# Six places for inputs instead of four in a fused attention, soft-MoE and gate kernel on one core

## The chip, the core and the metric

The kernel runs on one core of one Trainium2 chip. The metric is the device time of one execution in microseconds, as the median of several runs; lower is better. Before the change it is 154.87 us.

## The reference, cut to what matters

Three blocks follow each other: an attention between 512 tokens and 32 states per batch and head (both ways), a soft mixture of experts over all 4352 tokens, and a last block that changes only tokens whose skip score is above zero.

```python
scores = scale * np.matmul(x, state.transpose(0, 1, 3, 2))     # x: 8 batches, 8 heads, 512 x 64
xread = np.matmul(softmax(scores), state)
sread = np.matmul(softmax(scale * np.matmul(state, x.transpose(0, 1, 3, 2))), x)
...
d = softmax over tokens of (x @ phi)                            # phi: 512 x 32
slot_input = d.T @ x
h = np.maximum(slot_input[e] @ w1[e], 0.0)                      # w1: 8 x 512 x 1024
slot_out[e] = h @ w2[e]                                         # w2: 8 x 1024 x 512
out = softmax over slots of (x @ phi) @ slot_out
```

All data is float32. x is 8.4 MB, w1 and w2 are 16.8 MB each, and the output is 8.9 MB; so each byte of the 51.8 MB that cross the DMA queues crosses them once.

## The kernel before, in words

**Three parts.** The attention part handles eight batches, one after the other and interleaved. Then the first layer (`layer1`, line 691) multiplies the gathered slots with the eight `w1` weights, in two groups of four weights (`g` 0: weights 0 to 3, `g` 1: weights 4 to 7) and four quarters `kt` each; the second layer (`layer2`, line 775) does the same with `w2`, in sixteen units of 1 MB; and `combine` (line 805) and `store` (line 830) make and write the output.

**The order is written out by hand.** `ORDER` (line 556) is a list of steps, each a name with a batch or weight and a half, quarter or head; every engine gets its instructions in the order of that list. `A` are the transposes of an input on TensorE and `evA` their eviction, `Sc` the scores, `Tr`, `Er` and `aTr` other transposes, `R` the state's read (the last step of a batch that reads its input), `Lg` and `G` the logits and the gathering, `Bc` and `Dr` small transposes; `evS`, `sp`, `addT`, `mnT`, `sumT`, `evR` run on VectorE, `exS`, `exE`, `exT`, `evA` on ScalarE, `subT`, `nrmT`, `mvR` on GpSimd. `ldx.b.h` loads four heads of input b (0.5 MB), `ldw.n.q` quarter q of first-layer weight n (0.5 MB), `ldv` and `ldv2` units or half units of `w2`.

**All loads stand on one queue.** SyncE issues every load in the list's order. An issue waits until the place that it writes is free, and what stands behind it waits too. Each issue also waits for the completion of the issue eight before it, so that at most eight transfers are under way.

**Places.** An input takes 2048 words per partition. Inputs have four places: `XA` and `XB` in the working memory, and the two halves of the region of weight 7 (`w67[:, 4096:8192]`).

```python
w1s = [at(4096 * n, 4096) for n in range(6)] + [w67[:, 0:4096], w67[:, 4096:8192]]
xslot = [0, 1, 2, 3, 0, 1, 2, 0]
base = [XB, XT0, S0, XA, STT0, A0]        # w2 units 0 to 5
```

So input 4 waits for `R.0`, input 5 for `R.1`, input 6 for `R.2` and input 7 for `R.4`; weight 7 is loaded when inputs 6 and 3 are done. The first six units of `w2` go to the attention's working memory (`base`) as it comes free, the other ten where the first layer has used up quarters of `w1` (`w2u`, line 176).

Of the kernel before, what the change touches and what calls it, by code (L numbers as in the profile page):

```python
# [17 lines left out]
def kernel(  # L18
# [535 lines left out]


    ORDER = """
        ldsb.1.0 ldsb.0.0 warm.7.0 cp.0.0 cp.1.0 ST.1.0 cp.0.1 ldx.0.6 cp.1.1 ldx.0.0 ST.1.1 ldx.0.2 ST.0.0 phi.0.0
        ST.0.1 ldx.1.0 evST.1.0 evST.1.1 A.0.0 evST.0.0 A.0.3 evST.0.1 A.0.1 A.0.2 evA.0.3.dve evA.0.0.act
        evA.0.2.act Q.0.0 evA.0.1.act sh.0.0 ldx.1.4 sh.1.0 evsh.0.0 evQ.0.0 Sc.0.0 A.1.0 A.1.1 evS.0.0 evA.1.0.act
        evS.0.1 sp.0.1 ldx.2.4 A.1.2 sp.0.0 evA.1.1.act ldx.2.0 Bc.0.0 evsh.1.0 ldx.3.4 evB.0.0 Tr.0.1 A.1.3 Tr.0.0  # L560
        evA.1.2.act exE.0.1 evA.1.3.act addT.0.1 exE.0.0 Q.1.0 Sc.1.0 exS.0.1 R.0.0 mnT.0.1 ldx.3.0 evQ.1.0 addT.0.0
        mnT.0.0 ldx.4.0 exS.0.0 evS.1.1 A.2.0 sp.1.1 evS.1.0 subT.0.1 subT.0.0 A.2.1 exT.0.1 A.2.2 exT.0.0
        evA.2.1.act evA.2.0.act Bc.1.0 sp.1.0 evA.2.2.act A.2.3 sumT.0.0 Tr.1.0 evB.1.0 sumT.0.1 evA.2.3.act exS.1.0
        Tr.1.1 eps.0.0 rec.0.0 nrmT.0.0 ldx.4.4 A.3.0 Sc.2.0 A.3.2 exS.1.1 nrmT.0.1 addT.1.1 evR.0.0 evA.3.0.act
        mnT.1.1 evS.2.0 aTr.0.0 ldw.4.0 ldw.5.0 evA.3.2.act A.3.3 aTr.0.1 evaT.0.0 evS.2.1 addT.1.0 sp.2.0
        evA.3.3.act Bc.2.0 evaT.0.1 evB.2.0 A.3.1 mnT.1.0 subT.1.1 subT.1.0 Lg.0.0 ldw.3.0 A.4.0 sp.2.1 evA.3.1.act
        exE.1.0 exT.1.1 exE.1.1 exT.1.0 evL.0.0 Tr.2.0 Sc.3.0 sumT.1.1 R.1.0 exL.0.0 sumT.1.0 eps.1.0 ldw.0.0 Tr.2.1
        ldw.2.0 evA.4.0.act ldw.6.0 Dr.0.0 exS.2.0 rec.1.0 A.4.1 evD.0.0 nrmT.1.0 exS.2.1 ldw.1.0 A.4.2 evR.1.0
        nrmT.1.1 ldx.5.4 ldw.1.1 evA.4.1.act G.0.0 evS.3.0 evA.4.2.act evS.3.1 addT.2.1 mnT.2.1 ldx.5.0 evG.0.0
        addT.2.0 aTr.1.0 subT.2.1 evaT.1.0 aTr.1.1 evaT.1.1 A.4.3 evA.4.3.act RT.0.0 Bc.3.0 evB.3.0 evRT.0.0 mnT.2.0  # L570
        Lg.1.0 ldw.6.1 Sc.4.0 evL.1.0 sp.3.1 ldw.3.1 A.5.2 exT.2.1 sp.3.0 Tr.3.1 exE.2.0 Tr.3.0 subT.2.0 exL.1.0
        Dr.1.0 exT.2.0 exE.2.1 exS.3.1 A.5.0 sumT.2.1 A.5.1 mvR.0.0 sumT.2.0 eps.2.0 rec.2.0 evD.1.0 nrmT.2.1
        ldw.5.1 exS.3.0 ldw.0.1 nrmT.2.0 R.2.0 evA.5.2.act G.1.0 evA.5.0.act ldx.6.0 evA.5.1.act ldw.4.1 A.5.3
        evS.4.1 sp.4.1 evR.2.0 evS.4.0 addT.3.1 evG.1.0 aTr.2.1 evA.5.3.act ldx.6.4 aTr.2.0 evaT.2.1 ldw.2.1
        evaT.2.0 Tr.4.1 Lg.2.0 exS.4.1 mvR.1.0 mnT.3.1 Bc.4.0 addT.3.0 subT.3.1 exT.3.1 A.6.0 mnT.3.0 evL.2.0
        ldw.4.2 sp.4.0 exL.2.0 evB.4.0 Dr.2.0 sumT.3.1 subT.3.0 exT.3.0 sumT.3.0 eps.3.0 evD.2.0 rec.3.0 nrmT.3.0
        exE.3.0 Sc.5.0 exE.3.1 G.2.0 R.3.0 ldw.2.2 RT.1.0 nrmT.3.1 evG.2.0 addT.4.1 evA.6.0.act Tr.4.0 mnT.4.1
        ldw.6.2 ldw.3.2 RT.2.0 evRT.1.0 aTr.3.0 aTr.3.1 evR.3.0 ldw.1.2 A.6.3 addT.4.0 ldw.0.2 evRT.2.0 exS.4.0
        mnT.4.0 evaT.3.0 subT.4.1 evaT.3.1 evS.5.0 exT.4.1 Lg.3.0 sp.5.0 ldw.5.2 subT.4.0 exE.4.0 evL.3.0 exL.3.0
        Tr.5.0 exT.4.0 Dr.3.0 evS.5.1 Bc.5.0 sumT.4.1 evD.3.0 exE.4.1 evB.5.0 sumT.4.0 mvR.2.0 evA.6.3.act A.6.2  # L580
        exS.5.0 eps.4.0 R.4.0 rec.4.0 G.3.0 nrmT.4.0 sp.5.1 addT.5.0 ldx.7.4 evA.6.2.act ldx.7.0 nrmT.4.1 A.6.1
        Tr.5.1 evG.3.0 evA.6.1.act exS.5.1 aTr.4.0 mnT.5.0 addT.5.1 RT.3.0 mnT.5.1 aTr.4.1 evaT.4.0 Sc.6.0 subT.5.0
        evaT.4.1 exT.5.0 evR.4.0 Lg.4.0 evRT.3.0 A.7.3 evS.6.0 evS.6.1 evL.4.0 exE.5.0 subT.5.1 sp.6.1 exT.5.1
        sumT.5.1 A.7.2 A.7.1 exL.4.0 sumT.5.0 Dr.4.0 eps.5.0 Tr.6.1 mvR.4.0 exE.5.1 mvR.3.0 Bc.6.0 rec.5.0 evD.4.0
        nrmT.5.0 evA.7.2.act sp.6.0 A.7.0 R.5.0 evB.6.0 evA.7.1.act G.4.0 ldw.3.3 evR.5.0 ldw.0.3 Tr.6.0 addT.6.1
        ldw.2.3 ldw.5.3 mnT.6.1 ldw.4.3 nrmT.5.1 addT.6.0 evA.7.3.act evA.7.0.act ldw.1.3 mnT.6.0 exS.6.1 RT.5.0
        aTr.5.0 subT.6.1 evRT.5.0 exS.6.0 RT.4.0 ldw.6.3 mvR.5.0 aTr.5.1 Sc.7.0 evaT.5.0 evaT.5.1 Lg.5.0 exT.6.1
        evS.7.0 evL.5.0 Ls.0.0 exE.6.0 evS.7.1 Tr.7.0 evRT.4.0 evLs.0.0 ldv.4.0 exL.5.0 exE.6.1 sumT.6.1 subT.6.0
        Dr.5.0 exT.6.0 ldv.0.0 R.6.0 mnT.7.0 evD.5.0 sumT.6.0 evG.4.0 eps.6.0 ldw.7.0 ldw.7.1 rec.6.0 nrmT.6.0 G.5.0
        subT.7.0 ldw.7.2 ldw.7.3 exS.7.0 exS.7.1 warm.2.0 Tr.7.1 exT.7.0 Er.7.0 evR.6.0 mnT.7.1 RT.6.0 Er.7.1  # L590
        epsR.7.0 evE.7.0 subT.7.1 evE.7.1 evG.5.0 aTr.6.0 exT.7.1 R.7.0 recR.7.0 nrmT.6.1 evRT.6.0.dve sumT.7.0
        evR.7.0 mvR.6.0 sumT.7.1 epsT.7.0 aTr.6.1 epsT.7.1 recT.7.1 warm.4.0 recT.7.0 evaT.6.0 RT.7.0 nrmT.7.0.dve
        evaT.6.1 ldv2.2.0 Lg.6.0 nrmT.7.1 evRT.7.0 Ls.1.0 aTr.7.0 evLs.1.0 evL.6.0 evaT.7.0.dve ldv2.3.0 ldv2.4.1
        exL.6.0 aTr.7.1 mvR.7.0 Dr.6.0 LsT.0.0 evaT.7.1 evD.6.0 Lg.7.0 evL.7.0 exL.7.0 G.6.0 still.0.0 ldv2.5.0
        Dr.7.0 ldv2.2.1 evD.7.0 rowmax.0.0 G.7.0 exLs.0.0 still.0.0 exW.0.0 evG.6.0 esT.0.0 U.0.0 evG.7.0 ldv2.5.1
        evEs.0.0 U.1.0 sip0.0.0 wsg.0.0 ldv2.1.0 evU.0.0 evU.1.0 ldv2.1.1 SI.0.0 evSI.0.0 siT.0.0 evsi.0.0
# [462 lines left out]
```

## Time and profile before

| | |
|---|---|
| three runs | 154.41, 154.87, 155.14 us; median 154.87 us |
| profiled execution, its own time | 155.36 us |
| its span, first to last instruction | 153.5 us |
| PE, DVE, ACT, POOL busy | 130.0, 96.3, 84.8, 50.7 us |
| bytes moved, mean rate over the span | 51.84 MB, 338 GB/s |

The time of a run is that of the whole program; the span leaves out what lies ahead of the first and behind the last instruction, here 1.9 us. Starts in the rows are counted from the span's start. GB/s is what the core's 16 DMA engines moved together, and the DMA share is how busy they were on the mean; a share a little over 1 is a full stretch.

### The profile page before, as it was taken

To read this page: it belongs to the slowest core of one execution; us is meant where nothing else is said; L and a number is where in the kernel's file an instruction comes from. 1 tells how busy PE (TensorE), PEld (TensorE's weight loads), DVE (VectorE), ACT (ScalarE), POOL (GpSimd) and SP (SyncE) were. 2 spreads that over 40 slices of the span, in tenths; PEclk is the share of its full clock that TensorE was granted. 3 is DMA by queue.
4 is the path that set the end of the run, shared out by engine and by line. 5 is a ranking of instruction groups with operands and counts; after the bars stand their busy time and mean duration, and the time that the engine had idled before them with its cause. 6 is when DMAs were issued, how large, how long until landed. Compare 5 with 4: busy or idle time off the path is not lost.

```text
span 153.5 us, 4807 instructions
## 1 busy us (share of the span) xinstructions
PE 130.0 (85%) x1950; PEld 82.3 (54%) x1950; DVE 96.3 (63%) x230; ACT 84.8 (55%) x200; POOL 50.7 (33%) x89
## 2 busy tenths in 40 slices
...
PEclk9999999999999999999999999999999999999755
DMA  3999379999989999999899999999999689999980
GB/s 147 312 322 363 114 249 417 409 337 396 378 290 366 413 410 365 408 406 427 305 342 416 364 348 351 397 408 413 374 348 348 221 274 335 338 344 328 373 337 17
DMA packets 27916, 51.84 MB, mean 338 GB/s; under 512 B 2272, under 2 KB 19696, under 8 KB 27248
## 3 DMA queue, kind: packets, MB, share of 16 engines
...
HBM read 42.55 MB, written 8.91 MB: 335 GB/s over the span
## 4 chain that ended last, share of the span: by engine, by line
PE 51%; DMA 17%; DVE 14%; ACT 4%; issue 3%; POOL 2%; SPq 1%; ACTq 0%; DVEq 0%; POOLq 0%
PE b L243 11%; DMA mem<-in_x_dram 10%; PE b L784 7%; PE b L817 5%; PE pair L696 5%; PE b L696 5%; DMA mem<-in_moe_w_dram 4%; PE b L361 3%; DMA w<-in_x_dram 3%; PE pair L258 3%; DVE mem L266 3%; PE b L519 2%; DVE mem L319 2%; DVE mem L285 1%; PE b L719 1%
## 5 line engine op out<-in xcount | busy, mean ns | idle before, releaser
L239 ACT COPY mem<-b 128x512 f32<-128x512 f32 (+2 forms) x88 | 39.9, 506 | 23.4 <-PE b L797 7.9
L243 PE MATMUL b<-mem 128*128 128x128 f32 x240 | 34.1, 285 | 6.2 <-DMA mem<-in_x_dram 4.8
L243 PEld LDWEIGHTS b<-mem 128*128 128x128 f32 x240 | 27.6, 146 | 12.0 <-DMA mem<-in_x_dram 5.3
L327 POOL TENSOR_TENSOR mem<-mem 128x512 f32<-128x512 f32 x14 | 14.8, 1063 | 20.1 <-DVE mem L319 19.9
L347 POOL TENSOR_TENSOR mem<-mem 128x512 f32<-128x512 f32 x15 | 16.2, 1098 | 15.8 <-DVE mem L343 11.7
L784 PE MATMUL b<-mem 128*32 128x256 f32 (+1 forms) x208 | 16.4, 431 | 0.3
L784 PEld LDWEIGHTS b<-mem 128*32 128x32 f32 x208 | 6.7, 110 | 9.0 <-issue 4.8
L266 DVE TENSOR_SCALAR_CACHE_REDUCE mem<-pair 128x512 f32<-128x512 f32 x16 | 10.7, 680 | 1.4 <-PE pair L258 0.7
L817 PE MATMUL b<-mem 32*128 32x256 f32 (+1 forms) x72 | 11.3, 468 | 0.2
L331 ACT ACTIVATE mem<-mem 128x512 f32<-128x512 f32 x16 | 10.2, 640 | 2.0 <-POOL mem L327 1.2
L337 DVE TENSOR_REDUCE mem<-mem 128x16 f32<-128x512 f32 x16 | 10.4, 676 | 1.0 <-ACT mem L331 1.0
L300 DVE TENSOR_TENSOR mem<-b,mem 128x512 f32<-128x512 f32 x14 | 9.5, 678 | 1.1 <-ACT mem L307 0.6
L381 POOL COPY mem<-mem 32x128 f32<-32x128 f32 x32 | 9.7, 302 | 1.4
L319 DVE TENSOR_REDUCE mem<-mem 128x16 f32<-128x512 f32 x14 | 9.6, 684 | 0.4
L285 DVE TENSOR_SCALAR mem<-mem 128x512 f32<-128x512 f32 x14 | 9.1, 664 | 0.2
L278 ACT ACTIVATE mem<-mem 128x512 f32<-128x512 f32 x14 | 9.2, 661 | 0.0
L861 POOL TENSOR_TENSOR mem<-mem 128x512 f32<-128x512 f32 x1 | 1.3, 1265 | 23.1 <-issue 23.1
L258 PE MATMUL pair<-mem 64*32 64x256 f32 x256 | 8.9, 382 | 0.0
L307 ACT ACTIVATE mem<-b 128x512 f32<-128x512 f32 x14 | 8.4, 608 | 0.2
L817 PE MATMUL pair<-mem 32*128 32x256 f32 (+1 forms) x36 | 7.5, 491 | 0.9 <-DVE mem L825 0.5
L696 PE MATMUL pair<-mem 128*32 128x512 f32 x64 | 7.3, 595 | 0.6 <-issue 0.6
L828 ACT COPY mem<-b 128x256 f32<-128x256 f32 (+1 forms) x8 | 3.3, 426 | 8.1 <-PE pair L817 4.2
...
## 6 DMA issues: line engine op xcount, KB each, us to landing
...
```

The costliest lines, as they stand in the source:

```text
L239: (act.copy if eng == "act" else dve.tensor_copy)(dst, src)
L243: pe.transpose(out=t[:, 128 * m:128 * m + 128], in_=blk, identity=ident)
L258: pe.matmul(t[32 * q:32 * q + 32, j2, 256 * k:256 * k + 256], lhsT=stT[b // 4][64 * j2:64 * j2 + 64, h, 32 * (b % 4):32 * (b % 4) + 32], r ...
L266: dve.tensor_scalar(out=s_sb[k].rearrange("p (j m) -> p j m", j=2), in0=pair[:, :, 256 * k:256 * k + 256], scalar1=-scale, scalar2=None, o ...
L285: eng.tensor_scalar(out=s_sb[k], in0=s_sb[k], scalar1=b2[b % 2][:, k:k + 1], scalar2=None, op0=ALU.subtract)
L319: dve.tensor_reduce(out=mn[k], in_=t, axis=AX.X, op=ALU.min)
L327: pool.tensor_tensor(out=a3, in0=a3, in1=m3, op=ALU.subtract)
L337: dve.tensor_reduce(out=sm(b, k), in_=a_half(b, k)[1], axis=AX.X, op=ALU.add)
L347: eng.tensor_tensor(out=a3, in0=a3, in1=sm(b, k).unsqueeze(2).to_broadcast([P, 16, NS]), op=ALU.mult)
L696: pe.matmul(th[f2_][32 * c:32 * c + 32, :], lhsT=sip[:, 256 * kt + 64 * c + 32 * g:256 * kt + 64 * c + 32 * g + 32], rhs=w1s[n][:, 1024 * ...
L784: pe.matmul(ps[k][32 * c:32 * c + 32, cols], lhsT=hT[:, g, 4 * iq + i, 32 * c:32 * c + 32], rhs=w2s(4 * q4 + c, i, cols), start=(q8 == fir ...
L817: pe.matmul(ts[jj][:, 0:n], lhsT=c_of(b, j), rhs=so[32 * j:32 * j + 32, cols], start=True, stop=True)
```

## The change

Inputs get six places. The two new ones are the halves of the region of weight 6, `w67[:, 0:4096]`. Inputs 0 to 5 have a place each, input 6 takes that of input 0 and input 7 that of input 1. Weight 7 is loaded into the places of inputs 2 and 3 in two pairs of quarters (after `R.2` and `R.3`), weight 6 in those of inputs 4 and 5 (after `R.4` and `R.5`), behind all other first-layer weights. `w2` unit 0 lies where input 7 was, unit 3 where input 6 was.

```diff
--- before.py
+++ after.py
@@ -87,8 +87,8 @@
     XA, XB, XT0, S0, E2T0, A0 = W0, W0 + 2048, W0 + 4096, W0 + 6144, W0 + 7168, W0 + 8192
     STT0, SRT0, G0, ST0, R0 = W0 + 10240, W0 + 11264, W0 + 12288, W0 + 14336, W0 + 15360
     w1s = [at(4096 * n, 4096) for n in range(6)] + [w67[:, 0:4096], w67[:, 4096:8192]]
-    xbuf = [at(XA, 2048), at(XB, 2048), w67[:, 4096:6144], w67[:, 6144:8192]]
-    xslot = [0, 1, 2, 3, 0, 1, 2, 0]
+    xbuf = [at(XA, 2048), at(XB, 2048)] + [w67[:, o:o + 2048] for o in (4096, 6144, 0, 2048)]
+    xslot = [0, 1, 2, 3, 4, 5, 0, 1]
     xs = [xbuf[xslot[b]].rearrange("p (h j d) -> p h j d", h=H, j=J) for b in range(B)]
     xT = [at(XT0 + 512 * q, 512) for q in range(Q)]
     e2 = [at(XT0 + 512 * k, 512) for k in range(2)]
```

In `ORDER` the steps of the computation keep their order; only `ldx`, `ldw`, `ldv` and `ldv2` stand elsewhere. One line of the list that shows it, the first:

```diff
-        ldsb.1.0 ldsb.0.0 warm.7.0 cp.0.0 cp.1.0 ST.1.0 cp.0.1 ldx.0.6 cp.1.1 ldx.0.0 ST.1.1 ldx.0.2 ST.0.0 phi.0.0
+        ldsb.1.0 ldsb.0.0 ldx.0.6 ldx.0.0 ldx.0.2 phi.0.0 ldx.1.0 ldx.1.4 ldx.2.4 ldx.2.0 ldx.3.0 ldx.3.4 ldw.0.0
```

The instructions of VectorE, ScalarE and GpSimd are the same in both; those of TensorE differ only in the place from which an input is read. SyncE issues the same number of transfers, of the same sizes, in another order.

SyncE from the halves of inputs 2 and 3 on, before (`w67` is the region of weights 6 and 7, `mem` the rest; L196 is `load_x`, L204 `load_w1`; the trace calls the region `w`):

```order
L196 DMA w67_72<-in_x_dram 128x4x256 x4
L196 DMA mem_68<-in_x_dram 128x4x256 x2
L204 DMA mem_68<-in_moe_w1_dram 128x1024 x5
L204 DMA w67_72<-in_moe_w1_dram 128x1024
L204 DMA mem_68<-in_moe_w1_dram 128x1024
L196 DMA mem_68<-in_x_dram 128x4x256
L204 DMA mem_68<-in_moe_w1_dram 128x1024
L196 DMA mem_68<-in_x_dram 128x4x256
```

SyncE in the same stretch after the change, from the halves of inputs 2 and 3 to input 7:

```order
L196 DMA w67_72<-in_x_dram 128x4x256 x4
L204 DMA mem_68<-in_moe_w1_dram 128x1024 x2
L196 DMA w67_72<-in_x_dram 128x4x256 x2
L204 DMA mem_68<-in_moe_w1_dram 128x1024 x2
L196 DMA w67_72<-in_x_dram 128x4x256 x2
L204 DMA mem_68<-in_moe_w1_dram 128x1024 x4
L196 DMA mem_68<-in_x_dram 128x4x256 x2
L204 DMA mem_68<-in_moe_w1_dram 128x1024 x5
L196 DMA mem_68<-in_x_dram 128x4x256 x2
```

Before, the two halves of input 4 (the second line) stand ahead of every weight and wait for `R.0`. Now two weight quarters, input 4, two quarters, input 5 and four quarters follow at once, and the first issue that waits for a place is input 6.

SyncE from input 7 on to the last units of `w2` ahead of the first layer, before (L225 and L215 are `load_w2`, of half a unit and of a whole one; L218 is unit 6 and 7):

```order
L196 DMA mem_68<-in_x_dram 128x4x256 x2
L204 DMA mem_68<-in_moe_w1_dram 128x1024 x6
L204 DMA w67_72<-in_moe_w1_dram 128x1024
L225 DMA mem_68<-in_moe_w2_dram 128x1024
L215 DMA mem_68<-in_moe_w2_dram 128x2048
L204 DMA w67_72<-in_moe_w1_dram 128x1024 x4
L225 DMA mem_68<-in_moe_w2_dram 128x1024
L215 DMA mem_68<-in_moe_w2_dram 128x2048
L225 DMA mem_68<-in_moe_w2_dram 128x1024 x6
L218 DMA mem_68<-in_moe_w2_dram 128x4x512 x2
```

SyncE after the change, from input 7 to units 6 and 7 of `w2`:

```order
L196 DMA mem_68<-in_x_dram 128x4x256 x2
L204 DMA mem_68<-in_moe_w1_dram 128x1024 x11
L225 DMA mem_68<-in_moe_w2_dram 128x1024
L204 DMA w67_72<-in_moe_w1_dram 128x1024 x8
L225 DMA mem_68<-in_moe_w2_dram 128x1024 x2
L215 DMA mem_68<-in_moe_w2_dram 128x2048 x2
L225 DMA mem_68<-in_moe_w2_dram 128x1024 x5
L218 DMA mem_68<-in_moe_w2_dram 128x4x512 x2
```

Before, weight 7 came last and `w2` unit 0 ahead of it. Now eight quarters, of weight 7 and then 6, stand in one row ahead of all of `w2` but half of unit 4, and unit 0 (the second whole unit, L215) waits for `R.7`.

## Rows read from the trace of the kernel before

**Rows 1.** The page: the span in 40 slices, TensorE's clock, DMA share, rate.
```profile
PEclk9999999999999999999999999999999999999755
DMA  3999379999989999999899999999999689999980
GB/s 147 312 322 363 114 249 417 409 337 396 378 290 366 413 410 365 408 406 427 305 342 416 364 348 351 397 408 413 374 348 348 221 274 335 338 344 328 373 337 17
```

**Rows 2.** SyncE's queue in order of time: start, us, line, what, count.
```profile
5.80 5.02 SPq L196 DMA_DIRECT2D w<-in_x_dram  x4
...
17.70 2.23 SPq L196 DMA_DIRECT2D mem<-in_x_dram  x2
...
55.50 0.94 SPq L196 DMA_DIRECT2D mem<-in_x_dram  x2
...
72.93 2.48 SPq L204 DMA_DIRECT2D w<-in_moe_w_dram  x4
...
80.69 6.53 SPq L225 DMA_DIRECT2D mem<-in_moe_w_dram  x6
90.67 1.24 SPq L218 DMA_DIRECT2D mem<-in_moe_w_dram  x2
```

**Rows 3.** Windows: stretch, us, busy of PE, PEld, DVE, ACT, POOL, clock, DMA, GB/s.
```profile
2.00:16.00 14.00, 13.71 (x158) 12.29 (x160) 7.29 (x23) 8.53 (x16) 1.16 (x2) 1.00 1.02 329
16.00:20.00 4.00, 3.55 (x110) 2.69 (x109) 3.89 (x9) 3.32 (x9) 2.11 (x2) 1.00 0.29 86
20.00:22.00 2.00, 2.00 (x18) 1.93 (x18) 1.93 (x5) 2.00 (x6) 0.00 (x0) 1.00 0.70 230
...
47.00:56.00 9.00, 8.11 (x207) 5.87 (x192) 8.31 (x20) 8.06 (x22) 5.87 (x9) 1.00 1.04 412
62.00:72.00 10.00, 9.35 (x169) 7.39 (x170) 6.14 (x17) 7.04 (x19) 5.67 (x10) 1.00 1.04 414
...
86.00:94.00 8.00, 6.95 (x124) 3.22 (x127) 3.98 (x11) 0.58 (x2) 2.94 (x9) 1.00 0.99 340
94.00:110.00 16.00, 16.00 (x152) 5.61 (x148) 10.70 (x18) 4.67 (x6) 0.15 (x2) 1.00 1.03 400
110.00:121.00 11.00, 10.74 (x150) 5.00 (x142) 0.43 (x1) 1.20 (x3) 0.00 (x0) 1.00 1.09 346
...
124.00:149.00 25.00, 17.04 (x141) 7.45 (x137) 13.34 (x29) 9.69 (x22) 5.26 (x9) 0.89 1.00 347
```

**Rows 4.** The chain that ended last, in order of time: start, us, what.
```profile
30.75 8.28 DMA mem<-in_x_dram
...
55.92 7.54 DMA mem<-in_x_dram
```

**Rows 5.** TensorE in order of time: start, us, line, count [idle before it <-releaser].
```profile
39.08 1.09 PE L243 MATMUL b<-mem 128*128 128x128 f32 x8 [1.85 <-DMA mem<-in_x_dram]
...
45.57 0.66 PE L243 MATMUL b<-mem,w 128*128 128x128 f32 x4 [0.63 <-DMA w<-in_x_dram]
...
62.01 1.09 PE L243 MATMUL b<-mem 128*128 128x128 f32 x8 [2.20 <-DMA mem<-in_x_dram]
63.60 0.63 PE L243 MATMUL b<-mem 128*128 128x128 f32 x4 [0.49 <-DMA mem<-in_x_dram]
...
89.56 1.93 PE L696 MATMUL pair<-mem 128*32 128x512 f32 x16 [0.63 <-issue]
```

**Rows 6.** VectorE in order of time, the same columns.
```profile
41.37 0.29 DVE L369 TENSOR_TENSOR mem<-b,mem 128x128 f32<-128x128 f32 x1 [1.73 <-PE b L361]
...
66.69 0.29 DVE L369 TENSOR_TENSOR mem<-b,mem 128x128 f32<-128x128 f32 x1 [3.23 <-PE b L361]
```

**Rows 7.** TensorE around the last transposes and reads of the attention part.
```profile
75.38 0.82 PE L243 MATMUL b<-mem 128*128 128x128 f32 x6
...
76.34 1.10 PE L361 MATMUL b<-mem 128*32 128x64 f32 x64
```

**Rows 8.** Waits: engine and line, waited for: us in total, times, longest.
```profile
PEld b L784 <- DMA mem<-in_moe_w_dram: 1.5, 3, 0.6
```

**Rows 9.** GpSimd in order of time, batch 5's normalization.
```profile
63.34 2.06 POOL L347 TENSOR_TENSOR mem<-mem 128x512 f32<-128x512 f32 x2 [0.83 <-DVE mem L343]
```

More of the change, by code (lines that the diff above doesn't have):

```diff
@@ L556 @@
     ORDER = """
-        ldsb.1.0 ldsb.0.0 warm.7.0 cp.0.0 cp.1.0 ST.1.0 cp.0.1 ldx.0.6 cp.1.1 ldx.0.0 ST.1.1 ldx.0.2 ST.0.0 phi.0.0
[L558 to L596, printed above, removed]
+        ldsb.1.0 ldsb.0.0 ldx.0.6 ldx.0.0 ldx.0.2 phi.0.0 ldx.1.0 ldx.1.4 ldx.2.4 ldx.2.0 ldx.3.0 ldx.3.4 ldw.0.0
@@ new lines @@
+        ldw.1.0 ldx.4.0 ldx.4.4 ldw.2.0 ldw.3.0 ldx.5.0 ldx.5.4 ldw.4.0 ldw.5.0 ldw.0.1 ldw.1.1 warm.7.0 cp.0.0
+        cp.1.0 ST.1.0 cp.0.1 cp.1.1 ST.1.1 ST.0.0 ST.0.1 evST.1.0 evST.1.1 A.0.0 evST.0.0 A.0.3 evST.0.1 A.0.1 A.0.2
+        evA.0.3.dve evA.0.0.act evA.0.2.act Q.0.0 evA.0.1.act sh.0.0 sh.1.0 evsh.0.0 evQ.0.0 Sc.0.0 A.1.0 A.1.1
+        evS.0.0 evA.1.0.act evS.0.1 sp.0.1 A.1.2 sp.0.0 evA.1.1.act Bc.0.0 evsh.1.0 evB.0.0 Tr.0.1 A.1.3 Tr.0.0
+        evA.1.2.act exE.0.1 evA.1.3.act addT.0.1 exE.0.0 Q.1.0 Sc.1.0 exS.0.1 R.0.0 ldx.6.0 ldx.6.4 ldw.2.1 ldw.3.1
@@ new lines @@
+        ldw.4.1 ldw.5.1 ldw.0.2 mnT.0.1 evQ.1.0 addT.0.0 mnT.0.0 exS.0.0 evS.1.1 A.2.0 sp.1.1 evS.1.0 subT.0.1
+        subT.0.0 A.2.1 exT.0.1 A.2.2 exT.0.0 evA.2.1.act evA.2.0.act Bc.1.0 sp.1.0 evA.2.2.act A.2.3 sumT.0.0 Tr.1.0
+        evB.1.0 sumT.0.1 evA.2.3.act exS.1.0 Tr.1.1 eps.0.0 rec.0.0 nrmT.0.0 A.3.0 Sc.2.0 A.3.2 exS.1.1 nrmT.0.1
+        addT.1.1 evR.0.0 evA.3.0.act mnT.1.1 evS.2.0 aTr.0.0 evA.3.2.act A.3.3 aTr.0.1 evaT.0.0 evS.2.1 addT.1.0
+        sp.2.0 evA.3.3.act Bc.2.0 evaT.0.1 evB.2.0 A.3.1 mnT.1.0 subT.1.1 subT.1.0 Lg.0.0 A.4.0 sp.2.1 evA.3.1.act
@@ new lines @@
+        exE.1.0 exT.1.1 exE.1.1 exT.1.0 evL.0.0 Tr.2.0 Sc.3.0 sumT.1.1 R.1.0 ldx.7.0 ldx.7.4 ldw.1.2 ldw.2.2 ldw.3.2
+        ldw.4.2 ldw.5.2 ldw.0.3 ldw.1.3 ldw.2.3 ldw.3.3 ldw.4.3 ldw.5.3 ldv.4.0 exL.0.0 sumT.1.0 eps.1.0 Tr.2.1
+        evA.4.0.act Dr.0.0 exS.2.0 rec.1.0 A.4.1 evD.0.0 nrmT.1.0 exS.2.1 A.4.2 evR.1.0 nrmT.1.1 evA.4.1.act G.0.0
+        evS.3.0 evA.4.2.act evS.3.1 addT.2.1 mnT.2.1 evG.0.0 addT.2.0 aTr.1.0 subT.2.1 evaT.1.0 aTr.1.1 evaT.1.1
+        A.4.3 evA.4.3.act RT.0.0 Bc.3.0 evB.3.0 evRT.0.0 mnT.2.0 Lg.1.0 Sc.4.0 evL.1.0 sp.3.1 A.5.2 exT.2.1 sp.3.0
@@ new lines @@
+        Tr.3.1 exE.2.0 Tr.3.0 subT.2.0 exL.1.0 Dr.1.0 exT.2.0 exE.2.1 exS.3.1 A.5.0 sumT.2.1 A.5.1 mvR.0.0 sumT.2.0
+        eps.2.0 rec.2.0 evD.1.0 nrmT.2.1 exS.3.0 nrmT.2.0 R.2.0 ldw.7.0 ldw.7.1 evA.5.2.act G.1.0 evA.5.0.act
+        evA.5.1.act A.5.3 evS.4.1 sp.4.1 evR.2.0 evS.4.0 addT.3.1 evG.1.0 aTr.2.1 evA.5.3.act aTr.2.0 evaT.2.1
+        evaT.2.0 Tr.4.1 Lg.2.0 exS.4.1 mvR.1.0 mnT.3.1 Bc.4.0 addT.3.0 subT.3.1 exT.3.1 A.6.0 mnT.3.0 evL.2.0 sp.4.0
+        exL.2.0 evB.4.0 Dr.2.0 sumT.3.1 subT.3.0 exT.3.0 sumT.3.0 eps.3.0 evD.2.0 rec.3.0 nrmT.3.0 exE.3.0 Sc.5.0
@@ new lines @@
+        exE.3.1 G.2.0 R.3.0 ldw.7.2 ldw.7.3 RT.1.0 nrmT.3.1 evG.2.0 addT.4.1 evA.6.0.act Tr.4.0 mnT.4.1 RT.2.0
+        evRT.1.0 aTr.3.0 aTr.3.1 evR.3.0 A.6.3 addT.4.0 evRT.2.0 exS.4.0 mnT.4.0 evaT.3.0 subT.4.1 evaT.3.1 evS.5.0
+        exT.4.1 Lg.3.0 sp.5.0 subT.4.0 exE.4.0 evL.3.0 exL.3.0 Tr.5.0 exT.4.0 Dr.3.0 evS.5.1 Bc.5.0 sumT.4.1 evD.3.0
+        exE.4.1 evB.5.0 sumT.4.0 mvR.2.0 evA.6.3.act A.6.2 exS.5.0 eps.4.0 R.4.0 ldw.6.0 ldw.6.1 rec.4.0 G.3.0
+        nrmT.4.0 sp.5.1 addT.5.0 evA.6.2.act nrmT.4.1 A.6.1 Tr.5.1 evG.3.0 evA.6.1.act exS.5.1 aTr.4.0 mnT.5.0
```

14 lines of the change are left out of this document (added).

## The prediction

> **What bounds the kernel now.** I began with the slices [rows 1]. TensorE's clock is granted in full until the last slices, where TensorE has nothing left to do, so the clock is no term. The DMA row is at 9 nearly all the way, with holes: the start, the fifth slice (15 to 19 us, 114 GB/s), and smaller ones later. The reader is to see that transfers fill almost the whole span, so a hole that is filled early can move everything behind it.
>
> Next the queue [rows 2] and the windows [rows 3]. Input 3 is issued by 10.8 us; then SyncE stands until 17.70, because input 4 needs the place of input 0. Meanwhile the queue runs dry: 86 GB/s from 16 to 20 us, 230 from 20 to 22, against 412 and 414 in two long stretches of weights. That hole is 4 us at 326 and 2 us at 182 GB/s missing, 1.7 MB or 4.1 us of transfers. It isn't on a computing engine's path at that moment. What it does is make everything behind it late.
>
> Then the chain [rows 4]: two of its long pieces before the first layer are transfers of inputs, 8.28 us (input 5, issued when `R.1` is done) and 7.54 us (input 7, when `R.4` is done). They are the length of a transfer with its queue, not the length of a stall. The stalls are on the engines: TensorE waits 1.85 us for input 5, 0.63 us for input 6, and 2.20 and 0.49 us for the two halves of input 7 [rows 5]. VectorE, behind it, stands 1.73 us at the first and 3.23 us at the last, with nothing at input 6 [rows 6]. The first layer starts at 89.56 us [rows 5].
>
> From there on transfers and TensorE run side by side: 400 GB/s from 94 to 110 us, 346 to 121, and then the stores at 347 to 149 [rows 3]. TensorE waits for `w2` in the second layer, but for 1.5 us only [rows 8]. So behind the first layer's start there are two limits within 2 us of each other, TensorE's own work and the transfers of `w2`, and the stores follow on whichever is later.
>
> **The change, part by part.**
>
> *Inputs 4 and 5 no longer wait for a place.* With 6 places they are issued behind input 3, each behind two weight quarters. Bytes up to the end of input 5: 0.6 of states and phi, 6.3 of inputs, 2.1 of weights, 9.0 MB. 4.8 MB have landed at 16 us [rows 3]; the other 4.2 MB at the lowest rate of these rows that is no hole, 329 GB/s, take 13 us, so input 5 lands by 29 us. It was wanted at 37.2 us (39.08 less 1.85). The stall goes. What counts of it is VectorE's 1.73 us: VectorE is what everything in this stretch passes through, and it goes on without a gap behind it.
>
> *Input 6 waits for `R.0`, input 7 for `R.1`.* Both reads end (by 17.7 us [rows 2] and 30.75 us [rows 4], when the issues behind them went out) before the queue, with eight transfers under way, can reach these issues, so they hold up nobody. Input 6: 9.0 MB, four more quarters (2.1) and itself (1.0) make 12.1 MB, by 38 us at 329 GB/s; it was wanted at 44.9. Input 7: with five quarters and itself 15.8 MB, by 49 us; wanted at 59.8. Both stalls go. Input 6 gives nothing, since VectorE had no gap there. Input 7's is worth at most 3.23 us (VectorE) and at least 2.20 (TensorE's first wait). I take 2.5: without it, `Dr.4` would be held by ScalarE's `exL.4`, some 0.2 us short of the full 2.69 us of TensorE's two waits. What is late next there is GpSimd: batch 5's normalization occupies it from 63.34 to 65.40 [rows 9], and the transposes `aTr.5` behind `R.5` need it. `R.5` would end near 64, so it just fits.
>
> Start of the first layer: 1.73 + 2.5 = **4.2 us earlier**, at 85.3 us.
>
> *Weight 6 last, in the places of inputs 4 and 5; weight 7 ahead of it.* Their issues wait for `R.2`, `R.3`, `R.4` and `R.5`. I cost these waits at nothing: by the queue's bytes they come up at about 50 to 60 us, near the reads themselves, with seven transfers (3.7 MB, 9 us) still under way as cover. `R.5`, which ended at 66.5 us and would end near 62, is the only one that SyncE really stands for. If that cover were gone, each us would come out of the queue. Weight 6 is needed in the second group of the first layer, and lands over 10 us before the first group begins (next paragraph).
>
> *The queue without the hole.* From 16 us on: inputs 4 to 7, 4.19 MB at 329 GB/s, 12.7 us; `w1` and half a unit of `w2`, 17.3 MB at 412, 42.0 us. So all that is free to go is in at 70.7 us. What is left of units 0 to 5 (5.77 MB) waits for the last batch: the first issue for `Er.7.1`, which ended near 75.9 us [rows 7] and moves to 71.7. After the wait for `R.0` the rate took some 2 us from the issue to come up [rows 2, 3], so transfers go on at about 73.2. `R.7` behind it (at 76.34 before) frees unit 0 in time. 5.77 MB at 412 are 14.0 us: they end at 87.2.
>
> *From there to the end.* The ten other units (10.49 MB) are issued from 1.1 us behind the first layer's start (90.67 against 89.56). Before, 11.2 MB were moved from 91 to 121 us (3 us at 340, 16 at 400, 11 at 346 GB/s), so 0.74 MB of older transfers, 2 us, stood ahead of them: they began at about 93. Now they begin at 87.2, which is later than the start of the first layer and 1.1 us (86.4). The transfers thus come **5.8 us** earlier, TensorE's own work 4.2 us, and 1.5 us of its waits for `w2` can go: TensorE at most 5.7 us. Two limits that meet leave some waiting at the seam; I leave a third of the 1.5 us and take **5.2 us**. Stores start that much earlier; they fill the queue at 347 GB/s [rows 3] and stay as long as they are.
>
> **Sum.** 1.73 + 2.5 + 1.0 = 5.2 us off the profiled execution: 155.36 to 150.2. Off the median, which lies 0.5 us lower: 154.87 - 5.2 = **149.7 us**. Bounds of the terms: 1.7 to 1.85, 2.2 to 3.2, 0 to 1.5, or 3.9 to 6.6 us.
>
> **A rule against it.** In 9 and 10 us stretches of weights the queue ran at 412 and 414 GB/s [rows 3]. The page "DMA: Bandwidth & Descriptors" of the Trainium skill (Where 436 GB/s comes from) says that the memory's share for one core, about 358 GB/s, binds transfers from memory; the trace goes past that, so I don't use it. By that figure the 27.3 MB from 16 us to the end of unit 5 would take 76 us and end at 92, 1 us before they do now, and the time would stay near 154.
>
> **The rivals.**
>
> *Less: the freed stalls fall to something else.* GpSimd's normalization [rows 9], or ScalarE's evictions, take input 7's place as the last to end, and half or more of the 2.5 us stays. For it: GpSimd is within 1 us of being the last. Against: it has a 0.83 us gap ahead of it, and it moves with VectorE when input 5's stall goes. Gain 1.7 to 3.5 us; 152.3 us.
>
> *Nothing: the issues come no earlier, or the tail is the bound.* If eight transfers under way or the waits for `R.2` to `R.5` hold the queue, the holes only change place; or the 5.77 MB behind `Er.7.1` set the end as before. A third way to it: the queue without gaps runs at some 354 GB/s, between the 329 and 340 of some stretches and the 412 of others [rows 3]; then the 27.3 MB from 16 us on end at 93 us, as before. This is where the page's figure above would lead. For it: before, some 6 MB were still to move at that point too (the four quarters issued from 72.93 us and eight transfers of `w2` [rows 2]). Against: eight transfers are 10 us of work, more than any wait here but one, and 412 and 414 GB/s are no short peaks. 154.9 us.
>
> *Slower: the queue without gaps runs slower.* Rows of inputs are short, and the early stretch with them shows 329 GB/s; 86 to 94 us, at a full DMA share, shows 340 [rows 3]. If mixed inputs and weights, side by side with all engines, run at that rate, the 27.3 MB from 16 us on end at 16 + 80 = 96 us, where they ended at 93: 3.3 us slower, 158.2 us. It decides below 27.3 MB / 77 us = 354 GB/s. Against: 412 and 414 GB/s with all engines busy.
>
> **How the numbers follow.** The forecast, with 3.5 to 7.3 us off (147.6 to 151.4), has 0.65; less 0.17; nothing 0.10; slower 0.08. About 0.8 us (0.5%) can be told from no change. Of "less", nearly all is beyond that: faster 0.82, same 0.10, slower 0.08. For 8 in 10 the range takes the forecast and most of "less": 147.4 to 153.6.
>
> **What would show it.** Right: no hole between 16 and 22 us in the DMA row; SyncE issuing weights from about 11 us on; no wait of TensorE for an input behind 30 us, and VectorE's gaps of 1.73 and 3.23 us gone; the first layer at 85 to 86 us; TensorE's wait for `w2` under 1 us. Wrong: the first layer still at 88 or later with the inputs long in place (then another engine binds), a queue below 360 GB/s between 20 and 60 us, or a hole of more than 3 us ahead of `Er.7.1`.

## The result, and the profile after

The changed kernel takes 150.32 us (median of 4 runs, 150.22 to 150.88) against 154.99 us beside it: a ratio of 0.9713, 95% interval 0.9678 to 0.9748, or 3.9 to 5.0 us less. Ratios, here and below, go by a kernel's fast runs alone (within 1.5% of its fastest), medians by all runs. The forecast was 5.2 us less, 149.7 us. The profiled execution took 150.22 us in place of 155.36, 5.1 us less; its span is 148.4 us.

The page's slices, beside [rows 1]:

```profile
PEclk9999999999999999999999999999999999999855
DMA  4899999999999999999699999999999499999980
GB/s 147 277 344 357 380 362 387 382 385 369 407 381 392 403 413 407 406 407 406 190 378 406 394 354 389 405 408 408 358 348 352 147 330 331 342 345 342 363 352 15
```

The hole in the fifth slice is gone. A new one stands in the twentieth (70 to 74 us, 190 GB/s). The hole ahead of the stores (slice 32 in both) is the old one, come earlier.

SyncE's queue, beside [rows 2], from inputs 2 and 3 on:

```profile
5.80 4.63 SPq L196 DMA_DIRECT2D w<-in_x_dram  x4
10.48 1.85 SPq L204 DMA_DIRECT2D mem<-in_moe_w_dram  x2
12.38 1.60 SPq L196 DMA_DIRECT2D w<-in_x_dram  x2
...
54.20 9.27 SPq L204 DMA_DIRECT2D w<-in_moe_w_dram  x8
71.94 0.80 SPq L225 DMA_DIRECT2D mem<-in_moe_w_dram  x2
...
86.58 1.24 SPq L218 DMA_DIRECT2D mem<-in_moe_w_dram  x2
...
117.39 1.28 SPq L833 DMA_DIRECT2D out_dram<-mem  x2
```

Weights go out from 10.48 us and input 4 from 12.38, where it was 17.70. The eight quarters of weights 7 and 6 are issued by 63.5 us; then SyncE stands until `Er.7.1` is done, 71.94. The first store stood at 122.15 us and stands at 117.39.

Windows, beside [rows 3], the columns as there:

```profile
16.00:20.00 4.00, 3.89 (x115) 2.96 (x112) 3.90 (x8) 3.32 (x9) 2.11 (x2) 1.00 1.05 388
...
22.00:50.00 28.00, 26.35 (x521) 19.64 (x523) 26.13 (x59) 25.92 (x68) 18.52 (x24) 1.00 1.05 387
50.00:70.00 20.00, 19.05 (x410) 14.06 (x410) 17.61 (x46) 18.96 (x51) 13.93 (x25) 1.00 1.03 407
70.00:75.00 5.00, 5.00 (x102) 4.41 (x104) 4.99 (x13) 4.27 (x10) 3.20 (x6) 1.00 0.73 234
```

The mixed queue of inputs and weights runs at 387 GB/s, weights alone at 407. From 70 to 75 us 0.87 MB are missing at that rate, or 2.1 us.

VectorE at the two places of [rows 6], then TensorE at the first layer [rows 5]:

```profile
39.92 0.28 DVE L369 TENSOR_TENSOR mem<-b,mem 128x128 f32<-128x128 f32 x1
...
62.76 0.29 DVE L369 TENSOR_TENSOR mem<-b,mem 128x128 f32<-128x128 f32 x1 [0.75 <-PE b L361]
```

```profile
85.46 1.92 PE L696 MATMUL pair<-mem 128*32 128x512 f32 x16 [0.63 <-issue]
```

The gap of 1.73 us is gone and that of 3.23 is down to 0.75. The first layer starts 4.10 us earlier. No wait of TensorE for an input is left but one of 0.6 us at the start, for input 0; its waits for `w2` are 1.0 us in place of 1.5 [rows 8], just at the bound that was named as a sign of being right:

```profile
PEld b L784 <- DMA mem<-in_moe_w_dram: 1.0, 2, 0.6
PE b L243 <- DMA mem<-in_x_dram: 0.6, 1, 0.6
```

### The profile page after: what moved, and what is told of

Same layout as the page of the kernel before. It is cut to its first block, busy times and chain, and to the rows that moved or that the text cites. A ratio compares the mean times of both kernels' runs of the same rounds, so it can differ in the third digit from the quotient of the medians.

```text
span 148.4 us, 4814 instructions
## 1 busy us (share of the span) xinstructions
PE 129.3 (87%) x1950; PEld 82.0 (55%) x1950; DVE 96.0 (65%) x230; ACT 84.3 (57%) x200; POOL 50.7 (34%) x89
## 4 chain that ended last, share of the span: by engine, by line
PE 39%; DVE 19%; DMA 18%; ACT 7%; POOL 5%; issue 4%; SPq 1%; ACTq 0%; DVEq 0%; POOLq 0%
DMA mem<-in_moe_w_dram 14%; PE b L243 10%; PE b L817 5%; PE pair L258 4%; DMA mem<-in_x_dram 4%; POOL mem L347 4%; PE pair L696 4%; DVE mem L266 4%; PE b L784 3%; DVE mem L285 3%; DVE mem L319 2%; ACT mem L239 2%; DVE mem L337 2%; PE b L361 2%; PE b L430 1%
## 5 line engine op out<-in xcount | busy, mean ns | idle before, releaser
L243 PE MATMUL b<-mem 128*128 128x128 f32 x224 | 32.1, 284 | 2.2 <-DVE mem L285 0.8
L243 PEld LDWEIGHTS b<-mem 128*128 128x128 f32 x224 | 25.7, 146 | 7.2 <-POOL mem L347 2.2
L243 PE MATMUL b<-mem,w 128*128 128x128 f32 x64 | 9.2, 277 | 0.0
L243 PEld LDWEIGHTS b<-mem,w 128*128 128x128 f32 x64 | 7.1, 140 | 1.5 <-issue 1.0
```

Source lines behind the costliest of these rows:

```text
L243: pe.transpose(out=t[:, 128 * m:128 * m + 128], in_=blk, identity=ident)
```

## The experiments

Two times tell where a run was won or lost: the start of the first layer (T1) and the first store. They are read from TensorE's and SyncE's rows as above, of one profiled execution of each kernel. Ratios are to the kernel before, run beside it on the same chip; its median was 153.9, 155.0 and 154.8 us on three chips, and its runs spread from 151.5 to 156.9 us there, so T1 and the store say more than the ratio where a us matters. Its own two profiled executions (155.4 and 155.9 us) are among its longer ones; what a short one gains by the change, no trace shows.

| kernel | median us | ratio, 95% interval | T1 | first store | store less T1 |
|---|---|---|---|---|---|
| before | 154.99 | | 89.56 | 122.15 | 32.6 |
| changed | 150.32 | 0.9713, 0.9678 to 0.9748 | 85.46 | 117.39 | 31.9 |
| four places, filled | 158.12 | 1.0176, 1.0094 to 1.0258 | 93.01 | 125.95 | 32.9 |
| input 7 late | 151.23 | 0.9831, 0.9751 to 0.9911 | 85.94 | 118.06 | 32.1 |
| tail filled | 150.02 | 0.9771, 0.9721 to 0.9822 | 85.59 | 116.71 | 31.1 |
| hole, no stall | 155.61 | 1.0161, 1.0099 to 1.0223 | 85.12 | 122.93 | 37.8 |
| changed, again | 150.34 | 0.9742, 0.9676 to 0.9808 | 84.94 | 116.81 | 31.9 |
| tail filled, again | 150.10 | 0.9727, 0.9658 to 0.9797 | 85.31 | 116.52 | 31.2 |
| input 5 late | 153.94 | 0.9977, 0.9925 to 1.003 | 89.44 | 121.36 | 31.9 |
| places alone | 150.91 | 0.9782, 0.9691 to 0.9874 | 85.92 | 117.81 | 31.9 |
| input 7 later still | 153.30 | 0.9964, 0.9911 to 1.0017 | 88.71 | 120.91 | 32.2 |
| before, again | 154.95 | 0.9984, 0.99 to 1.0068 | 88.94 | 122.49 | 33.6 |

The theory: two limits set the end. One is T1, which inputs set by coming late; the other is the queue's sum of transfers, which holes make longer; behind the first layer they meet. The rivals: Q, the queue's holes alone; E, the engines' waits for inputs alone; P, the new order of the transfers.

The diffs show the load steps of `ORDER` alone, in their order; the steps of the computation keep theirs in all kernels.

**Four places, with the first hole filled.**

```diff
-ldx.4.0 ldx.4.4 ldw.4.0 ldw.5.0 ldw.3.0 ldw.0.0 ldw.2.0 ldw.6.0 ldw.1.0 ldx.5.4 ldw.1.1 ldx.5.0
+ldw.4.0 ldw.5.0 ldw.3.0 ldw.0.0 ldx.4.0 ldx.4.4 ldw.2.0 ldw.6.0 ldw.1.0 ldw.1.1 ldw.6.1 ldw.3.1 ldw.5.1 ldx.5.4 ldw.0.1 ldx.5.0
...
```

> The kernel before with its four places; only the first hole of the queue is filled: four weight quarters go ahead of input 4, and as many weights as before stand between inputs 4, 5, 6 and 7. Theory (two limits: when inputs come decides the first layer's start, and the queue without holes decides the rest): input 5 lands near 37 us and input 7 near 61 us, so one to two of the 4.1 us of the first layer's start come back; start at 87.5 to 89 us, time 152.5 to 154.2 us. Rival Q (only the queue's holes count): the 4 us hole of 16 to 22 us is gone and the time falls to 150.5 to 151 us. Rival E (only the engines' waits for inputs count): as the theory says for the start, and the time follows the start one to one.

Measured: 158.12 us (156.2 to 159.5; the profiled execution is the longest). From 16 to 20 us the queue moves 398 GB/s, the hole is gone. And the kernel is slower, with T1 at 93.01. TensorE's waits for inputs and its first layer, then windows, in which the third figure from the end is the granted clock:

```profile
38.28 2.82 PE L243 MATMUL b<-mem 128*128 128x128 f32 x12 [2.66 <-DMA mem<-in_x_dram]
...
64.74 2.67 PE L243 MATMUL b<-mem 128*128 128x128 f32 x12 [2.92 <-DMA mem<-in_x_dram]
...
93.01 1.93 PE L696 MATMUL pair<-mem 128*32 128x512 f32 x16 [0.63 <-issue]
```

```profile
16.00:20.00 4.00, 3.81 (x113) 2.87 (x111) 3.90 (x8) 3.32 (x9) 2.11 (x2) 1.00 1.06 398
...
38.00:41.00 3.00, 2.72 (x13) 2.64 (x13) 0.37 (x2) 0.71 (x2) 2.34 (x3) 0.50 1.04 393
65.00:69.00 4.00, 4.00 (x23) 3.70 (x21) 0.48 (x2) 0.96 (x3) 2.06 (x2) 0.57 0.85 335
68.00:71.00 3.00, 3.00 (x85) 2.42 (x84) 0.50 (x2) 2.61 (x6) 0.00 (x0) 0.92 0.20 75
75.00:77.00 2.00, 1.92 (x78) 1.48 (x76) 2.00 (x6) 1.69 (x7) 0.86 (x1) 1.00 0.00 0
```

Input 5 still waits for `R.1` (issued at 29.82, before at 29.56), but now it stands behind more weights, so its first half lands later and not earlier: the twelve transposes that begin with it start at 38.28 us, before at 35.57. With input 7 it is the same (64.74 against 62.01). Rival Q falls: the early hole as such wasn't what the kernel paid for. The time alone would not show that, since the queue loses its lead again at 68 to 77 us, where it stands for places that the last batches free late (the last two windows); T1 does. My expectation fell too: I thought that a fuller queue would bring inputs earlier. What I hadn't expected at all is the clock (below).

**Input 7 late, in the changed kernel.**

```diff
-ldx.7.0 ldx.7.4 ldw.1.2 ldw.2.2 ldw.3.2 ldw.4.2 ldw.5.2 ldw.0.3 ldw.1.3 ldw.2.3 ldw.3.3 ldw.4.3
+ldw.1.2 ldw.2.2 ldw.3.2 ldw.4.2 ldw.5.2 ldw.0.3 ldw.1.3 ldw.2.3 ldw.3.3 ldx.7.0 ldx.7.4 ldw.4.3
```

> The changed kernel with input 7's two halves moved behind nine weight quarters, so that they land near 60 to 61 us; the queue stays full and its order is otherwise kept. Theory: TensorE waits for input 7 again, 2 to 3 us, the first layer starts at 87.5 to 88.4 us in place of 85.5, time 152.3 to 153.2 us. Rival Q: the queue has no new hole, so 150.3 us. Rival E: as the theory.

Measured: input 7 came a little earlier than I had reckoned, and TensorE waited 1.20 us:

```profile
59.39 1.53 PE L243 MATMUL b<-mem 128*128 128x128 f32 x12 [1.20 <-DMA mem<-in_x_dram]
```

```profile
63.38 0.29 DVE L369 TENSOR_TENSOR mem<-b,mem 128x128 f32<-128x128 f32 x1 [1.53 <-PE b L361]
```

VectorE's gap at `R.5` is 1.53 us in place of 0.75, T1 85.94 against 85.46 (0.70 us later when counted from the first score matmuls, 10.74 here and 10.96 there), and the time 151.23 us. So 0.4 us of such a wait is covered, and nearly all of the rest comes out at T1. The dose was too small to tell theory from rival by time alone; the next two were larger.

**Input 7 later still.**

```diff
-ldx.7.0 ldx.7.4 ldw.1.2 ldw.2.2
+ldw.1.2 ldw.2.2
...
-ldw.4.3 ldw.5.3 ldv.4.0
+ldw.4.3 ldw.5.3 ldx.7.4 ldx.7.0 ldv.4.0
```

> The changed kernel with input 7 behind all weights of this group; by the run with input 7 late it lands near 62 us and TensorE stands 3.5 to 4 us for it. Theory C (a wait of over 2.5 us also costs TensorE's clock: it stood at 0.5 for about 3.5 us behind the waits of 2.66 and 2.92 us in the run with four places and the filled queue, and stayed at 1.0 behind 1.85 and 2.20 us in the kernel before): the clock falls, and the first layer starts 4.5 to 6 us later than in the changed kernel. Without the clock: 3 to 3.5 us later. The time follows the start within 1 us in both.

Measured: 153.30 us, T1 88.71.

```profile
60.40 2.65 PE L243 MATMUL b<-mem 128*128 128x128 f32 x12 [2.17 <-DMA mem<-in_x_dram]
```

```profile
66.17 0.29 DVE L369 TENSOR_TENSOR mem<-b,mem 128x128 f32<-128x128 f32 x1 [4.30 <-PE b L361]
```

```profile
61.00:65.00 4.00, 4.00 (x32) 3.47 (x34) 0.84 (x3) 1.25 (x4) 2.06 (x2) 0.59 1.03 409
```

The wait was 2.17 us, not 3.5 to 4, and the clock fell all the same: the twelve transposes behind it took 2.65 us, where they took 1.53 with input 7 late. VectorE's gap is 4.30 us, 3.55 more than in the changed kernel; 2.17 less the 0.4 covered is 1.8, so the other 1.8 us is the clock's. TensorE's rows say the same: from the end of the wait to the first matmul of `R.5` it is 4.44 us here (60.40 to 64.84) and 2.66 with input 7 late (59.39 to 62.05). T1 is 3.3 us later and the store 3.5. That is the range which I gave for no fall of the clock; a smaller wait and the fall together led to it. Theory C falls in its bound, for a wait of less than 2.5 us was enough here.

**Input 5 late.**

```diff
-ldx.5.0 ldx.5.4 ldw.4.0 ldw.5.0 ldw.0.1 ldw.1.1 ldx.6.0 ldx.6.4 ldw.2.1 ldw.3.1 ldw.4.1
+ldw.4.0 ldw.5.0 ldw.0.1 ldw.1.1 ldx.6.0 ldx.6.4 ldw.2.1 ldx.5.4 ldw.3.1 ldx.5.0 ldw.4.1
```

> The changed kernel with input 5 issued behind input 6 and two weight quarters, so that its halves land near 38.5 and 40 us in place of 29. Theory: TensorE waits 2 to 3 us for input 5, the first layer starts 1.5 to 2.5 us later than in the changed kernel, and the time is 1.5 to 2.5 us longer, since behind it TensorE and the transfers start from there. If TensorE's clock falls behind a wait of over 2.5 us, as in the run with four places and the filled queue, 1 to 2 us more. Rival Q: no change.

Measured: 153.94 us, T1 89.44, 4.0 to 4.5 us later than in the two runs of the changed kernel.

```profile
38.18 0.66 PE L243 MATMUL b<-mem,w 128*128 128x128 f32 x4 [3.28 <-DMA w<-in_x_dram]
...
40.91 1.82 PE L243 MATMUL b<-mem,w 128*128 128x128 f32 x8 [0.47 <-DMA w<-in_x_dram]
...
89.44 1.92 PE L696 MATMUL pair<-mem 128*32 128x512 f32 x16 [0.63 <-issue]
```

```profile
39.00:42.00 3.00, 2.53 (x13) 2.13 (x12) 1.19 (x3) 2.09 (x6) 2.35 (x5) 0.51 1.03 396
72.00:77.00 5.00, 5.00 (x151) 4.19 (x153) 4.93 (x10) 4.40 (x12) 2.66 (x5) 1.00 0.13 20
```

The wait is 3.75 us, more than the 2 to 3 that I expected, and the clock is halved behind it. The price is most of the gain of the change (3.6 of 4.6 us in the medians on this chip), for one late input. How much of that is the clock's in the median is not shown: the profiled execution took 154.84 us at a mean granted clock of 0.951, while seven of the ten runs have 0.968 to 0.978, no less than the changed kernel's own (0.959 to 0.976), and still take 153.2 to 154.6. The second window shows where the queue's lead goes: the weights are in on time, the places of `w2` are not free before `Er.7.1`, and the queue stands for 5 us. This hole is a consequence of the late batch. Rival Q falls here again: the edit leaves no hole at input 5 (396 GB/s), and the store follows T1 to 0.1 us.

**A hole without a late input.**

```diff
-ldx.5.4 ldw.4.0 ldw.5.0 ldw.0.1 ldw.1.1 ldx.6.0 ldx.6.4 ldw.2.1 ldw.3.1 ldw.4.1 ldw.5.1 ldw.0.2 ldx.7.0 ldx.7.4 ldw.1.2
+ldx.5.4 ldx.6.0 ldx.6.4 ldx.7.0 ldx.7.4 ldw.7.0 ldw.7.1 ldw.4.0 ldw.5.0 ldw.0.1 ldw.1.1 ldw.2.1 ldw.3.1 ldw.4.1 ldw.5.1 ldw.0.2 ldw.1.2
...
-ldv.4.0 ldw.7.0 ldw.7.1 ldw.7.2
+ldv.4.0 ldw.7.2
```

> The changed kernel with a hole of its own and no late input: inputs 6 and 7 follow input 5 at once, then weight 7's first two quarters, which wait for R.2 (39.5 us), then all the other weights. The queue runs dry from about 34 to 41 us, some 6 us; no input comes late. Theory: the first layer still starts at 85.3 to 85.7 us, and the hole, less the 2.7 us that the queue has to spare at 70 to 75 and 88 us, comes out at the end: 3 to 4 us, time 153 to 154.5 us, with TensorE waiting for w2 or weight 6 instead. Rival Q: 6 us, 156 us. Rival E: no change, 150.3 us.

Measured: 155.61 us with T1 at 85.12.

```profile
30.00:44.00 14.00, 12.59 (x212) 9.48 (x209) 13.21 (x30) 12.89 (x37) 10.84 (x16) 1.00 0.53 167
44.00:87.00 43.00, 40.03 (x803) 28.59 (x803) 33.78 (x89) 32.04 (x87) 26.20 (x49) 1.00 1.03 410
```

```profile
85.12 1.92 PE L696 MATMUL pair<-mem 128*32 128x512 f32 x16 [0.68 <-DVE mem L548]
...
109.25 0.62 PE L784 MATMUL b<-mem 128*32 128x256 f32 x2 [0.99 <-DMA mem<-in_moe_w_dram]
111.96 8.18 PE L784 MATMUL b<-mem 128*32 128x256 f32 x90 [2.09 <-DMA mem<-in_moe_w_dram]
```

```profile
122.93 1.28 SPq L833 DMA_DIRECT2D out_dram<-mem  x2
```

```profile
PEclk9999999999999999999999999999857999999855
```

The hole is larger than I meant it to be: at 410 GB/s, 14 us with 167 lack 8.3 us of transfers. Less the 2.7 us to spare that is 5.6, and the store comes 5.5 us later than in the changed kernel (122.93 against 117.39). TensorE waits in the second layer, for `w2`, in place of the attention part. Rival E falls: with no late input and an early T1 the kernel is no faster than the one before. The last load ends in the 122nd us, in the changed kernel in the 117th, so the queue accounts for most of it. One thing stands beside it: the clock fell here too (the slices; from 111 to 118 us, behind the waits of 0.99 and 2.09 us), so that 5.6 and 5.5 us agree so well is in part luck. The clock doesn't carry the result: seven of the ten runs have a mean granted clock of 0.965 or more, against 0.948 in the profiled one, and take 154.3 to 156.6 us. The mechanism was as the theory said; the size of the hole I had mis-set.

**Tail filled.**

```diff
-ldv2.1.0 ldv2.2.0 ldv2.3.0 ldv.0.0
+ldv2.3.0 ldv2.2.0 ldv2.1.0 ldv.0.0
```

> The changed kernel with units 3 and 2 of w2 issued ahead of unit 1's first half, so that the queue does not stand until Er.7.1: the hole of 70 to 75 us (2.2 us of transfers) shrinks by 1 to 2 us. Theory: behind 86.6 us the transfers wait for the first layer anyway, so the filled hole opens again there; time 150.0 to 150.4 us. Rival Q: 148.5 to 149.5 us. Rival E: no change.

> Units 3 and 2 of w2 ahead of unit 1's first half, once more beside the changed kernel. Theory (two limits): the hole only moves to 86 to 89 us, and what is won is at most the small rest of TensorE's wait for w2 in the second layer: 0 to 0.5 us less than the changed kernel. Rival Q (the queue's holes count): 2 us less.

> The changed kernel itself, on the chip of the other runs of this call, as their measure. All theories: first layer at 85.3 to 85.6 us, time 150.0 to 150.6 us.

Measured: 150.02 us, and 150.10 beside 150.34 of the changed kernel on the same chip (whose T1 of 84.94 is 0.4 us below what I expected of it). The first run's windows:

```profile
70.00:75.00 5.00, 5.00 (x99) 4.39 (x98) 4.96 (x14) 4.09 (x9) 3.21 (x6) 1.00 1.02 397
86.00:89.00 3.00, 3.00 (x30) 1.03 (x26) 1.02 (x4) 0.00 (x0) 0.00 (x0) 1.00 0.56 141
```

The queue is full from 70 to 75 us (397 GB/s in place of 234) and stands from 86 to 89 (141). The hole moved, as the theory said, to where `w2` waits for the first layer. The second layer's waits shrink (store less T1 is 31.1 and 31.2 in place of 31.9), but 0.2 us in the median beside the changed kernel is inside the spread; this version isn't shown to beat the changed kernel.

**Places alone.**

```diff
-ldw.0.0 ldw.1.0 ldx.4.0 ldx.4.4 ldw.2.0 ldw.3.0 ldx.5.0 ldx.5.4 ldw.4.0 ldw.5.0 ldw.0.1
+ldx.4.0 ldx.4.4 ldw.4.0 ldw.5.0 ldw.3.0 ldw.0.0 ldw.2.0 ldw.1.0 ldx.5.4 ldw.1.1 ldx.5.0 ldw.3.1
...
```

> The six places alone: the transfers keep the order in which the kernel before issues them, but for weight 6, which must come last now, and unit 0 of w2. Theory: with a free place nothing holds inputs 4 and 5, so the queue has no hole and no input is late; the same time as the changed kernel within 0.5 us. Rival P (the new order of the transfers is what brings the gain): 1 us or more slower than the changed kernel.

Measured: 150.91 us, 0.6 more than the changed kernel on the same chip, where I had allowed 0.5; T1 85.92, store less T1 31.9. The first score matmuls and `evR.5`, in this kernel, then the first score matmuls in the changed one (its `evR.5` is above) and in the kernel before:

```profile
11.39 1.22 PE L258 MATMUL pair<-mem 64*32 64x256 f32 x32
...
63.20 0.29 DVE L369 TENSOR_TENSOR mem<-b,mem 128x128 f32<-128x128 f32 x1 [0.76 <-PE b L361]
```

```profile
10.96 1.22 PE L258 MATMUL pair<-mem 64*32 64x256 f32 x32
```

```profile
10.62 1.21 PE L258 MATMUL pair<-mem 64*32 64x256 f32 x32
```

From the first score matmul to `evR.5` it is 51.81 us here, 51.80 in the changed kernel, 51.81 in its second run (10.12 to 61.93). So these runs differ up to there by when the first score matmuls start, ahead of which all kernels issue the same loads, and the new order of the transfers gives the first layer nothing beyond what the places give. Rival P falls for the order of inputs and first-layer weights, the part that is put back here. Behind it `w2` and weights 7 and 6 stand in the order of the changed kernel, so what their order gives by itself (store less T1 is 31.9 here, 32.6 in the kernel before) is not tested.

**The kernel before once more.**

> The kernel before itself, for its trace on the chip of these runs: all theories say 151.5 to 156.5 us. Theory C says that runs with a longer time show TensorE's clock at 0.5 behind a wait for input 5 or 7, and runs without such a stretch lie near 152 to 155 us.

Measured: 154.95 us (152.4 to 156.4). In its profiled execution TensorE waits 1.37, 0.62, 1.59 and 0.49 us for inputs 5, 6 and 7 and the clock stays full; T1 is 88.94. A fallen clock makes no part of that run, though it is among the longer ones (155.9): theory C falls here too. Over the 53 runs of this kernel beside the others, the 19 with a mean granted clock of 0.962 or less are 1.2 to 1.8 us longer on the mean of their chip than the rest, so the clock may have a part in the spread, but the rest alone spreads from 151.5 to 156.9 us. What spreads it stays open. It goes with late loads: the kernels in which TensorE waits for none of the later inputs and the queue has no made hole spread by 0.7 to 1.5 us, the others by 2.3 to 5.0 (but the kernel before in its first four runs by 0.7).

## Why the prediction was right

*Inputs 4 and 5.* Issued as said; VectorE's 1.73 us gap is gone entirely. `evR.2` stands 1.45 us earlier (39.92 against 41.37) and not 1.73, because the first score matmuls began 0.34 us later in this execution (10.96 against 10.62). The working had 4.8 MB landed at 16 us; by [rows 3] it is 4.6 (14 us at 329 GB/s), which moves no term.

*Input 6, input 7.* Nothing and 2.5 us, as said: the gap went from 3.23 to 0.75 us. The reason for 2.5 and not 2.69 was right too: `Dr.4` (L421) now waits for ScalarE's `exL.4` (L415), 0.27 us where 0.2 was said:

```profile
60.08 0.33 PE L421 MATMUL b<-mem 128*128 128x128 f32 x1 [0.27 <-ACT mem L415]
```

The runs with input 7 late show that this term is the input's arrival and no other edit. T1: 4.2 us forecast, 4.10 measured; counted from the first score matmul, 4.44. That T1 fits to 0.1 us is partly luck: the two terms, measured from one `evR` to the next, give 4.3 us, the stretch from `evR.5` to T1 was 0.2 us shorter, and the later start took 0.3 back.

*Weights 6 and 7 at nothing.* The eight issues went out over 9.27 us from 54.20 on, and the queue moved 407 GB/s from 50 to 70 us meanwhile, so the cover held.

*The queue without the hole.* "All that is free to go is in at 70.7 us": the rate falls in the 71st us (340, then 205 GB/s). The forecast took inputs at 329 and weights at 412 GB/s, 393 on the mean; measured are 387 for the mixture and then 407 for weights alone. The page "DMA: Bandwidth & Descriptors" of the Trainium skill (Where 436 GB/s comes from) has about 358 GB/s for transfers from memory to one core; 48 us above it, in stretches without a break, go against that here, and so the rivals of a queue at 354 GB/s or less fall.

*From there to the end.* This is the term that was too large. I had the transfers 5.8 us earlier and TensorE's waits for `w2` down by 1.0 us. Summed over windows of 1 us, what goes ahead of the ten last units (all 42.8 MB of loads less their 10.49) was in at about 93.6 us before and at 88.8 now, 4.8 us earlier and not 5.8; the last load ends in the 122nd us before and in the 117th now. The stand at 70 to 75 us isn't the reason, for the forecast had it (70.7 to 73.2). What it lacked is mainly a slower start behind the stand (193, then 324 GB/s from 73 to 75 us, where I had 412 from 73.2 on) and a dip at 88 us, where units 6 and 7 had only just been issued (86.58):

```profile
73.00:74.00 1.00, 1.00 (x33) 0.91 (x22) 1.00 (x5) 0.83 (x2) 0.77 (x3) 1.00 0.86 193
74.00:75.00 1.00, 1.00 (x14) 0.83 (x15) 0.99 (x4) 0.89 (x3) 0.00 (x0) 1.00 0.90 324
...
88.00:89.00 1.00, 1.00 (x16) 0.32 (x12) 1.00 (x3) 0.00 (x0) 0.00 (x0) 1.00 0.83 211
```

TensorE's stretch of second-layer matmuls up to the low half's end went from 9.87 to 9.21 us:

```profile
105.40 9.21 PE L784 MATMUL b<-mem 128*32 128x512 f32 x128
```

That is 0.66 us, not 1.0. So the first store came 4.10 + 0.66 = 4.76 us earlier, and the span 5.1 with some 0.3 us in the stores. The medians moved by 4.7 us: the profiled execution of before lay 0.4 us above its median, and of the changed kernel 0.1 us below.

*Where the view of the hole was wrong.* "What it does is make everything behind it late." The run with four places says otherwise: with the same hole filled with weights, inputs came later still. The kernel before had slack in the queue at that point, for its weights are wanted only at T1. What the change removes is the wait for a place; that the hole goes with it is a second gain, needed because T1 comes earlier and the queue must keep up, as the run with a hole and no late input shows. (The "some 6 MB" of the second rival are 6.8 by the sizes of the issues; no term hangs on it.)
